# Linformer attention and a squared-ReLU layer: the attention of the next batch in three pieces instead of four, a projection moved up, loads issued earlier

## The chip, the cores and the metric

The kernel runs on one core of a Trainium2 chip. The metric is the device time of one execution in microseconds (us). The kernel before takes 484.29 us, the median of 4 runs (483.24 to 484.89).

## What is computed

Inputs are q, k, v of 8 batches x 8 heads x 1024 rows x 64, two projection matrices E and F (64 x 1024), and the weights of a two-layer network (512 x 2048 and 2048 x 512), all float32.

```python
k_proj = np.einsum('ks,bhsd->bhkd', E, k)
v_proj = np.einsum('ks,bhsd->bhkd', F, v)
scores = scale * np.matmul(q, k_proj.transpose(0, 1, 3, 2))
scores = scores - np.max(scores, axis=-1, keepdims=True)
attn = np.exp(scores)
attn = attn / (np.sum(attn, axis=-1, keepdims=True) + 1e-09)
attn_out = np.matmul(attn, v_proj)
...
x = np.ascontiguousarray(attn_out.transpose(0, 2, 1, 3)).reshape(B * S, H * D)
h = np.maximum(x @ w_in, 0.0)
return (h * h @ w_out).astype(np.float32)
```

Keys and values are projected from 1024 rows to 64, so attention is small: nearly all matmul work is in the two products of the network, over 8192 rows.

## The kernel before

**The network sets the frame.** For each of the 8 batches, `ffn_groups` returns a list of small functions, "groups", which the main loop at the end calls one after the other. A batch's 1024 rows go in two chunks. A chunk's first product (16 groups, line 489) multiplies xT by w_in into PSUM tiles; ScalarE takes the relu (lines 543 and 545), VectorE squares it into `hsq` (line 553). Its second product (line 509) is done with a scheme of seven block products instead of eight: p1 to p7, each 256 columns wide, with combined weights T1 to T4 and combined operands `s` (VectorE, line 503). Products gather in two PSUM accumulators called y and x/z; ScalarE copies partial results out (line 633), VectorE adds them into the output tile `o_sb` (line 639), and SP stores it. In batches 2 to 6, groups 0 to 15 are the first product of chunk 0, 16 to 30 its second product in the order p1a, p2a, p1b, p1c, p2b, p6, p5, p7, p3, p4 (from p6 on, two groups each), 31 to 46 the first product of chunk 1, and 47 to 61 its second. `before` says how many of the eight products of p2 go into p2a, ahead of p1b; the rest are p2b. z takes the bank of x in these batches, and p6 and p7 take that of y.

**Attention rides between the groups.** The attention of batch b+1 is cut into steps, and a table says ahead of which group of batch b each step is issued: BATCH_1 while batch 0 runs, BATCH_2 while batch 1 runs, PIECES after that. Scores (line 234, four matmuls on 64-row tiles that share the array) go to a PSUM tile; ScalarE takes their exponentials (line 241); sums and values (line 249) are matmuls on 64x32 tiles; logs and inverses (lines 261, 264) give 1/sum on ScalarE; normalize (line 274) writes xT on VectorE. The projection of K and V (lines 207 and 208) fills all 128 rows; its result is copied out by `copy_kp` (VectorE, two copies, and a transposing DMA on SP that makes kT), `copy_vp` (ScalarE, two copies) and `copy_v_down` (VectorE). `transpose_q` is a transposing DMA on SP that makes qT. A second set of tables, AHEAD and AHEAD_1, places projection, copies and transpose_q of the batch after the next.

**Order and buffers.** Each engine executes its instructions in the order in which the program issues them, waiting only on data and on buffers. From batch 2 on, PSUM holds three attention tiles of two banks each, which scores, sums, values and every second first-product tile take in turn, and two single banks, which the other first-product tiles and y, x/z take in turn. K_sb, V_sb, Q_sb and qT have one buffer each, the other projection results two, the output tiles two. Loads are issued on GpSimd (line 108) and change the type from float32 to bfloat16 on the way; transposes and stores are issued on SP. Both queues are executed in order. A load waits until the buffer's last reader is done.

**Where loads stand.** The main loop calls `load_batch(b + 2)` ahead of group 35 of batch 0, 14 of batch 1, and 1 of the others; batch 1's loads are at group 31 of batch 0. The order is Q, K, V but for batch 1.

Of the kernel before, what the change touches and what calls it, by code (L numbers as in the profile page):

```python
# [8 lines left out]
P = 128  # L9
F32 = mybir.dt.float32  # L10
BF16 = mybir.dt.bfloat16
# [9 lines left out]
def kernel(  # L21
# [13 lines left out]
    B, H, S, D = q.shape  # L35
    KP = E.shape[0]
    C = H * D
# [5 lines left out]
    NCB = C // P  # L43
    NFB = FF // P
    HFB = NFB // 2
    NT = NI // 2
# [14 lines left out]
    x_pool = ctx.enter_context(tc.tile_pool(name="x", bufs=2))  # L61
# [17 lines left out]
    def regroup_psum():  # L79
        mixed_stack.close()  # L80
        ffn_home.clear()
        for pool in mixed:
            ffn_pools.remove(pool)
        att_pools.append(mixed_stack.enter_context(psum_pool("mps", 1)))

    def att_psum(shape, dtype):
        pool = att_pools.pop(0)
        att_pools.append(pool)
        return pool.tile(shape, dtype, tag="att", name="ps_att")

    def ffn_psum(name, shape=(P, 512), dtype=F32):

        pool = ffn_home[name] = ffn_pools[0]
        used(name)
        return pool.tile(list(shape), dtype, tag="ffn", name=name)

    def used(name):
        pool = ffn_home.get(name)
        if pool:
            ffn_pools.remove(pool)  # L100
            ffn_pools.append(pool)
# [4 lines left out]
    def load(name, src, b):  # L106
        t = qkv_pool.tile([P, H, NI * D], BF16, name=name)
        nc.gpsimd.dma_start(t[:], rows(src, b))  # L108
        return t

    e_f32 = []
    for src in (E, F):
        t = relu_pool.tile([KP, S], F32, tag="h_relu", name="e_f32")
        nc.sync.dma_start(t[:], src[:])
        e_f32.append(t)
    K_first, V_first, Q_first = (
        qkv_pool.tile([P, H, NI * D], BF16, name=n) for n in ("K_sb", "V_sb", "Q_sb"))
# [46 lines left out]
    def E_and_F():  # L164
        for t, src, copy in ((ET, e_f32[0], nc.vector.tensor_copy), (FT, e_f32[1], nc.scalar.copy)):
            e_bf = soft_pool.tile([KP, S], BF16, tag="expT", name="e_bf")
            copy(e_bf[:], src[:])
            ps = ffn_psum("ps_E", (P, NI, KP), BF16)
            view = e_bf[:].rearrange("k (p i) -> k i p", i=NI)
            for i in range(NI):  # L170
                nc.tensor.transpose(ps[:, i, :], view[:, i, :], ident[0:KP, 0:KP])
            copy(t[:], ps[:])
# [7 lines left out]
    def combine_weights(q4, name):  # L180
        js = slice(4 * q4, 4 * q4 + 4)
        o, a, b = {"T1": (T1, W12, W11), "T2": (T2, W22, T1), "T3": (T3, W22, W12), "T4": (T4, W21, T2)}[name]
        nc.vector.tensor_tensor(out=o[:, js], in0=a[:, js], in1=b[:, js], op=ALU.subtract)
# [4 lines left out]
    class Attention:  # L188
# [2 lines left out]

        def __init__(self, b, Q, K, V):
            self.Q, self.K, self.V = Q, K, V
            self.xT = x_pool.tile([P, NCB, 2, NT, P], BF16, name="xT")
            self.exp, self.rs, self.ps = {}, {}, {}
            self.qT = qt_pool.tile([P, H * NT, P], BF16, name="qT")

        def transpose_q(self):
            nc.sync.dma_start_transpose(out=self.qT[:], in_=self.Q[:].rearrange("p h c -> p (h c)"))

        def project(self, early=0):
            ps = self.ps["kv"] = ffn_psum("ps_kv") if early else att_psum([P, C], F32)
            kv = self.K[:].rearrange("p h (i d) -> p h i d", i=NI)
            vv = self.V[:].rearrange("p h (i d) -> p h i d", i=NI)
            for i in range(NI):
                f, l = i == 0, i == NI - 1
                nc.tensor.matmul(ps[0:KP, :], lhsT=ET[:, i, :], rhs=kv[:, :, i, :], start=f, stop=l)  # L207
                nc.tensor.matmul(ps[KP:P, :], lhsT=FT[:, i, :], rhs=vv[:, :, i, :], start=f, stop=l)
# [62 lines left out]
            self.ps["v", g, e] = self.quads(g, lambda o, h: self.vp[o, h, e, :])  # L271

        def normalize(self, g, e):
            nc.vector.tensor_tensor(  # L274
                out=self.xT[:, 2 * g + e].rearrange("p a n t -> p a (n t)"),
                in0=self.ps["v", g, e][:], in1=self.rs[g][:], op=ALU.mult,
            )
# [156 lines left out]

    PIECES = {
        18: "scores 0, scores 1, scores 2", 20: "exponentials 0, exponentials 1", 21: "exponentials 2",
        23: "scores 3, exponentials 3",
        27: "sums 0, sums 1, values 0 0, reciprocals 0", 28: "reciprocals 1", 29: "normalize 0 0",  # L440
        49: "values 0 1, values 1 0, values 1 1", 51: "normalize 0 1", 53: "normalize 1 0",
        55: "normalize 1 1",
    }

    AHEAD = {23: "project", 24: "copy_kp", 25: "copy_vp", 26: "copy_v_down", 33: "transpose_q"}
    AHEAD_1 = {33: "transpose_q", 53: "project 1", 58: "copy_kp", 59: "copy_vp", 61: "copy_v_down"}
    BATCH_1 = {
        33: "project 1", 34: "copy_kp, transpose_q, copy_vp", 37: "copy_v_down",
# [7 lines left out]
    BATCH_2 = {  # L456
        12: "project 1", 13: "copy_kp, transpose_q", 14: "copy_vp", 17: "copy_v_down",
# [5 lines left out]
    }  # L463
    SECOND_HALF = {
# [16 lines left out]
    def calls(table, n):  # L481
        for c in filter(None, table.get(n, "").split(", ")):
            name, *args = c.split()
            yield name, [int(a) for a in args]

    def ffn_groups(b, xT):
# [30 lines left out]
        def chunk(ch):  # L517
# [93 lines left out]
            lo, hi = range(0, 4), range(4, 8)  # L611


            before = lo if b == B - 1 else range(3 if b == 1 else 2)

            ALL = slice(0, 2)

# [96 lines left out]
                    nc.sync.dma_start(out_rows[b, ch, 1, :, tb, 0:MH], st["o1"][:, tb, 0:MH])  # L714

            lohi = lambda p: [lambda: p(lo), lambda: p(hi)]
            if b == B - 1:
                (p5a, p5b), rest = lohi(p5), lohi(p7) + lohi(p3)
                second = [p1a, p2a, p5a, p1b, p1c, p2b] + lohi(p6) + [p5b] + rest
            elif b > 1:  # L720
                second = [p1a, p2a, p1b, p1c, p2b] + lohi(p6) + lohi(p5) + lohi(p7) + lohi(p3)
            else:
                second = [p1a, p2a, p1b, p1c] + lohi(p5) + lohi(p6) + lohi(p3) + lohi(p7) + [p2b]
            second += [p4_last] if last else lohi(p4)
            return steps, second, begin_sums, operands

        (f0, s0, begin0, operands0), (f1, s1, begin1, operands1) = chunk(0), chunk(1)
        if b:
            return f0 + s0 + f1 + s1
# [15 lines left out]


    with tc.manual_schedule(engines=ORDERED):
        def load_batch(b):

            if b < B:  # L750
                order = [("K_sb", k), ("V_sb", v), ("Q_sb", q)] if b == 1 else [("Q_sb", q), ("K_sb", k), ("V_sb", v)]
                t = {n: load(n, src, b) for n, src in order}
                return Attention(b, t["Q_sb"], t["K_sb"], t["V_sb"])

        E_and_F()
        cur = Attention(0, Q_first, K_first, V_first)
        cur.first_stages()
        nxt = ahead = None
        for b in range(B):
            for n, g in enumerate(ffn_groups(b, cur.xT)):  # L760
                if b == 0:
                    for name, args in calls(SECOND_HALF, n):
                        getattr(cur, name)(*args)
                    for name, args in calls(WEIGHTS, n):
                        combine_weights(args[0], name)
                    if n == 31:
                        nxt = load_batch(1)
                if nxt:
                    for name, args in calls((BATCH_1, BATCH_2, PIECES)[min(b, 2)], n):
                        getattr(nxt, name)(*args)  # L770
                    if n == (35, 14, 1)[min(b, 2)]:
                        ahead = load_batch(b + 2)
                if b and ahead:
                    for name, args in calls(AHEAD_1 if b == 1 else AHEAD, n):
                        getattr(ahead, name)(*args)
                g()
            if b == 0:
                nxt.normalize(1, 1)
            if b == 1:
                regroup_psum()  # L780
            cur, nxt, ahead = nxt, ahead, None


# [28 lines left out]
```

The softmax here doesn't subtract the row's maximum and nothing guards it: scores larger than these inputs give would overflow.

## Time and profile before

The profiled execution took 484.71 us; its span, first to last instruction, is 482.9 us, with a granted TensorE clock of 1.000. The table adds rows of the page and of the groups by shape that the prediction does not show. Busy times of different engines overlap; idle is the time that the engine stood still just before these instructions.

| group | count | busy us | mean ns | idle before, us |
|---|---|---|---|---|
| first product, 128x512, both PSUM kinds (L489) | 1024 | 238.5 | 379 | 0.2 |
| scores (L234) | 112 | 9.0 | 389 | 0.1 |
| projection into an attention tile (L207, L208) | 64 | 15.4 | 382 | 0.0 |
| projection into a single bank (L207, L208) | 48 | 11.4 | 382 | 0.0 |
| values (L249, expT, vp) | 224 | 8.9 | 380 | 0.3 |
| squares on VectorE (L553) | 123 | 150.1 | 1223 | 79.8 |
| exponentials, 128x1024 (L241) | 28 | 27.5 | 1043 | 1.8 |
| loads of K, V, Q on GpSimd (L108) | 21 | 18.5 | 880 | mostly Q, 252.8, for the transpose of the Q before |

A matmul's mean is its latency; because matmuls overlap, what one costs in a stream is the distance between starts. In the list of DMAs, K takes a median of 14.8 us from issue to landing, V 21.7, Q 10.2, a store of 512 KB 3.2, a transpose of Q 7.7 and one of K 2.6. Batch 2's first product starts at 143.48 us, that of batch 3 at 200.63 and that of batch 4 at 257.77.

### The profile page before, as it was taken

The numbers are of one execution on the slowest core, as the hardware profiler recorded it, in microseconds if no ns is written. First come the engines' busy times: TensorE is split into PE (matmuls) and PEld (weight loads), VectorE is DVE, ScalarE is ACT, GpSimd is POOL, SyncE is SP. The second block draws the span as 40 slices with busy tenths as digits, with TensorE's granted clock in tenths as the row PEclk, the third lists the DMA queues.
The fourth block names the chain that finished last, engine by engine and source line by source line (L and its number), as shares of the span: only waits on it lengthen the run. The fifth ranks groups of instructions, "written<-read, shape, count | busy, mean of one in ns | idle before, by whom it ended". The sixth has DMA issues, their size and how long they took to land.

```text
span 482.9 us, 8401 instructions
## 1 busy us (share of the span) xinstructions
PE 470.4 (97%) x3630; PEld 294.1 (61%) x3630; DVE 314.6 (65%) x382; ACT 246.9 (51%) x365; POOL 34.9 (7%) x48
## 2 busy tenths in 40 slices
PE   3899999999999999999999999999999999999997
PEld 2544677475574756757476664846658475766656
DVE  1468955563967659584694937858486755949383
ACT  2377635758516574357633566155652666334352
POOL 6440020020020002000110002000000000000000
PEclk9999999999999999999999999999999999999999
DMA  9999989669989268900797027950521002020202
GB/s 153 203 204 207 158 186 194 148 108 212 172 142 239 34 164 133 228 1 12 174 173 178 0 65 132 197 143 1 132 54 65 24 1 88 1 89 0 88 1 87
DMA packets 72789, 55.46 MB, mean 115 GB/s; under 512 B 33968, under 2 KB 64944, under 8 KB 72752
## 3 DMA queue, kind: packets, MB, share of 16 engines
q0 software_dynamic: 30624, 29.36, 38.4%
q1 hardware_dynamic: 42128, 25.56, 20.3%
q8 instruction: 28, 0.46, 0.4%
q14 instruction: 9, 0.07, 0.1%
HBM read 59.24 MB, written 16.78 MB: 157 GB/s over the span
## 4 chain that ended last, share of the span: by engine, by line
PE 92%; DVE 4%; ACT 2%; DMA 2%; issue 0%; ACTq 0%; POOLq 0%
PE ps_h L489 27%; PE ps_y L509 21%; PE ps_att L489 17%; PE ps_z L509 15%; PE ps_att L509 2%; PE ps_att L249 2%; DMA K_sb<-in_k_dram 2%; PE ps_att L234 2%; PE ps_att L207 2%; DVE hsq L553 1%; PE ps_x L509 1%; DVE s L503 1%; PE ps_k L290 1%; PE ps_kv L207 1%; ACT h_relu L543 1%; DVE xT L274 0%
## 5 line engine op out<-in xcount | busy, mean ns | idle before, releaser
L553 DVE TENSOR_TENSOR hsq<-h_relu 128x1024 bf16<-128x1024 f32 x123 | 150.1, 1223 | 79.8 <-ACT h_relu L545 63.2
L489 PEld LDWEIGHTS <-w_in 128*128 128x128 bf16 x1024 | 99.7, 98 | 117.7 <-issue 1.9
L489 PE MATMUL ps_h<-xT,w_in 128*128 128x512 bf16 x640 | 147.8, 379 | 0.2 <-DVE xT L379 0.2
L509 PEld LDWEIGHTS <-s 128*128 128x128 bf16 x1024 | 98.8, 98 | 18.4 <-issue 6.5
L543 ACT ACTIVATE h_relu<-ps_h 128x512 f32<-128x512 f32 x159 | 92.4, 596 | 24.2 <-PE ps_h L489 23.9
L489 PE MATMUL ps_att<-xT,w_in 128*128 128x512 bf16 x384 | 90.7, 379 | 0.0
L509 PEld LDWEIGHTS <-hsq 128*128 128x128 bf16 x768 | 73.8, 98 | 18.1 <-issue 7.5
L545 ACT ACTIVATE h_relu<-ps_att 128x1024 f32<-128x1024 f32 x48 | 49.1, 1023 | 55.2 <-PE ps_att L489 55.2
L509 PE MATMUL ps_y<-T,s 128*128 128x256 bf16 x480 | 57.7, 273 | 0.1
L503 DVE TENSOR_TENSOR s<-hsq 128x1024 bf16<-128x1024 bf16 x64 | 43.6, 685 | 0.0
L274 DVE TENSOR_TENSOR xT<-ps_att,rs 128x1024 bf16<-128x1024 f32 x28 | 33.4, 1218 | 0.7 <-PE ps_att L249 0.7
L639 DVE TENSOR_TENSOR o_sb<-ps_z,p_b 128x512 f32<-128x512 f32 x16 | 11.1, 692 | 32.3 <-PE ps_z L509 27.2
L509 PE MATMUL ps_y<-w_out,hsq 128*128 128x256 bf16 x240 | 31.2, 273 | 0.0
L509 PE MATMUL ps_z<-T,s 128*128 128x256 bf16 x256 | 31.0, 273 | 0.0
L509 PE MATMUL ps_z<-w_out,s 128*128 128x256 bf16 x256 | 30.6, 273 | 0.0
L633 ACT COPY o_sb<-ps_y 128x512 f32<-128x512 f32 x15 | 8.7, 579 | 40.8 <-PE ps_y L509 40.6
L509 PE MATMUL ps_y<-T,hsq 128*128 128x256 bf16 x240 | 29.0, 273 | 0.0
L241 ACT ACTIVATE expT<-ps_att 128x1024 bf16<-128x1024 f32 x28 | 27.5, 1043 | 1.8 <-PE ps_att L234 1.8
L633 ACT COPY p_a<-ps_y 128x512 f32<-128x512 f32 x15 | 8.8, 586 | 32.1 <-PE ps_y L509 32.1
L108 POOL DMA_DIRECT2D Q_sb<-in_q_dram x7 | 6.1, 876 | 252.8 <-DMA qT<-Q_sb 251.6
L503 DVE TENSOR_TENSOR s<-s,hsq 128x1024 bf16<-128x1024 bf16 x32 | 21.9, 688 | 0.5
L503 DVE TENSOR_TENSOR s<-hsq,s 128x1024 bf16<-128x1024 bf16 x32 | 21.9, 686 | 0.0
(90 smaller groups left out, 284.6 us busy)
## 6 DMA issues: line engine op xcount, KB each, us to landing
out_dram<-o_sb SPq DMA_DIRECT2D x30, 512.0 KB, 3.2
K_sb<-in_k_dram POOLq DMA_DIRECT2D x7, 1024.0 KB, 14.8
V_sb<-in_v_dram POOLq DMA_DIRECT2D x7, 1024.0 KB, 21.7
Q_sb<-in_q_dram POOLq DMA_DIRECT2D x7, 1024.0 KB, 10.2
w_out<-in_moe_w_out_dram POOLq DMA_DIRECT2D x4, 512.0 KB, 13.2
w_in<-in_moe_w_in_dram POOLq DMA_DIRECT2D x7, 256.0 KB, 10.1
K_sb<-in_k_dram POOLq DMA_DIRECT2D x2, 512.0 KB, 9.1
out_dram<-o_sb SPq DMA_DIRECT2D x3, 256.0 KB, 2.1
```

Source lines behind the costliest of these rows:

```text
L207: nc.tensor.matmul(ps[0:KP, :], lhsT=ET[:, i, :], rhs=kv[:, :, i, :], start=f, stop=l)
L234: nc.tensor.matmul(ps[o, bank, :], lhsT=self.kT[r, 2 * pr + j, :], start=True, stop=True, rhs=self.qT[r, NT * (2 * pr + j):NT * (2 * pr + ...
L241: nc.scalar.activation(e[:], self.ps["s", pr][:], AF.Exp, scale=SCALE)
L274: nc.vector.tensor_tensor(out=self.xT[:, 2 * g + e].rearrange("p a n t -> p a (n t)"), in0=self.ps["v", g, e][:], in1=self.rs[g][:], op=AL ...
L489: nc.tensor.matmul(ps[:], lhsT=w_in_blk(cb, fb), rhs=xT[:, cb, :, 2 * ch:2 * ch + 2], start=(cb == 0), stop=(cb == NCB - 1),)
L503: nc.vector.tensor_tensor(out=s[o][:, js], in0=x, in1=y, op=op)
L509: nc.tensor.matmul(ps[tb] if len(ps) == 2 else ps[0][:, tb], lhsT=lhs[:, j, tb * P:(tb + 1) * P], rhs=rhs[:, j], start=first and n == 0 an ...
L543: nc.scalar.activation(r[:, n], ps[:], AF.Relu)
L545: nc.scalar.activation(r[:], st["h"][:], AF.Relu)
L553: multiply = lambda: nc.vector.tensor_tensor(out=o, in0=r[:], in1=r[:], op=ALU.mult)
L633: nc.scalar.copy(to[:, t], ps)
L639: nc.vector.tensor_tensor(out=to[:, t], in0=ps, in1=more[:, t], op=ALU.add)
```

## The change

The tables now name steps of two batches: a plain name is a step of batch b+1, a name with "+" one of batch b+2, and they replace AHEAD and AHEAD_1. Batches are kept in a dictionary. In the middle batches (2 to 5, table PIECES) scores 0 to 2, the projection for batch b+2 and scores 3 are all issued ahead of group 16, and the projection goes to a single bank instead of an attention tile; the copies follow there too, and transpose_q moves from group 33 to group 21. Batch 6 has its own table, LAST_PIECES, with the old places. In batches 2 to 5 the second product of chunk 0 starts p1a, p1b, p1c, p2a, p2b instead of p1a, p2a, p1b, p1c, p2b. In batch 1, values 1 and the projection move from group 53 to 55, and normalize 1 0 and 1 1 from 54 and 55 to 56 and 59. `before` is 4 instead of 2 in batch 0's second chunk and 4 instead of 3 in batch 1. Loads of batch 4 move to group 56 of batch 1, and those of b+3 to group 30 of batch b, in the order K, V, Q (Q, K, V for batches 2 and 3). xT and qT are taken from their pools when first written instead of with the load.

```diff
+        def begin_qT(self):
+            self.qT = qt_pool.tile([P, H * NT, P], BF16, name="qT")
+
+        def begin_xT(self):
             self.xT = x_pool.tile([P, NCB, 2, NT, P], BF16, name="xT")
...
         def transpose_q(self):
+            self.begin_qT()
             nc.sync.dma_start_transpose(out=self.qT[:], in_=self.Q[:].rearrange("p h c -> p (h c)"))
 
-        def project(self, early=0):
-            ps = self.ps["kv"] = ffn_psum("ps_kv") if early else att_psum([P, C], F32)
+        def project(self, in_ffn_bank=0):
+            ps = self.ps["kv"] = ffn_psum("ps_kv") if in_ffn_bank else att_psum([P, C], F32)
...
         def normalize(self, g, e):
+            if not self.xT:
+                self.begin_xT()
...
     PIECES = {
+        16: "scores 0, scores 1, scores 2, exponentials 0, +project 1, scores 3, exponentials 1, "
+            "+copy_vp, exponentials 2, +copy_kp",
+        19: "exponentials 3", 20: "+copy_v_down", 21: "+transpose_q",
+        27: "sums 0, sums 1, values 0 0, reciprocals 0", 28: "reciprocals 1", 29: "normalize 0 0",
+        49: "values 0 1, values 1 0, values 1 1", 51: "normalize 0 1", 53: "normalize 1 0",
+        55: "normalize 1 1",
+    }
+    LAST_PIECES = {
         18: "scores 0, scores 1, scores 2", 20: "exponentials 0, exponentials 1", 21: "exponentials 2",
         23: "scores 3, exponentials 3",
...
-    AHEAD = {23: "project", 24: "copy_kp", 25: "copy_vp", 26: "copy_v_down", 33: "transpose_q"}
-    AHEAD_1 = {33: "transpose_q", 53: "project 1", 58: "copy_kp", 59: "copy_vp", 61: "copy_v_down"}
...
-        30: "sums 0, sums 1, logs 0", 31: "logs 1", 33: "inverses 0",
-        36: "inverses 1", 47: "values 0 0, values 0 1", 48: "normalize 0 0, normalize 0 1",
-        53: "values 1 0, values 1 1", 54: "normalize 1 0", 55: "normalize 1 1",
+        30: "sums 0, sums 1, logs 0", 31: "logs 1", 
+        33: "+transpose_q, inverses 0", 36: "inverses 1", 47: "values 0 0, values 0 1", 48: "normalize 0 0, normalize 0 1",
+        55: "values 1 0, values 1 1, +project 1", 56: "normalize 1 0",
+        58: "+copy_kp", 59: "+copy_vp, normalize 1 1", 61: "+copy_v_down",
     }
...
-            before = lo if b == B - 1 else range(3 if b == 1 else 2)
+            before = range(2) if (b, ch) == (0, 0) or 1 < b < B - 1 else lo
...
-            if b == B - 1:
+            if 1 < b < B - 2 and ch == 0:
+                second = [p1a, p1b, p1c, p2a, p2b] + lohi(p6) + lohi(p5) + lohi(p7) + lohi(p3)
+            elif b == B - 1:
...
+                order = [("K_sb", k), ("V_sb", v), ("Q_sb", q)]
+                order = order[2:] + order[:2] if b in (2, 3) else order
                 t = {n: load(n, src, b) for n, src in order}
-                return Attention(b, t["Q_sb"], t["K_sb"], t["V_sb"])
+                batches[b] = Attention(b, t["Q_sb"], t["K_sb"], t["V_sb"])
+
+        LOADS = {0: {31: 1, 35: 2}, 1: {14: 3, 56: 4}}
...
+            tables = {0: BATCH_1, 1: BATCH_2, B - 2: LAST_PIECES, B - 1: {}}
+            for n, g in enumerate(ffn_groups(b, batches[b].xT)):
...
+                for name, args in calls(tables.get(b, PIECES), n):
+                    of = batches.get(b + (2 if name[0] == "+" else 1))
+                    if of:
+                        getattr(of, name.lstrip("+"))(*args)
+                if n in LOADS.get(b, {30: 0}):
+                    load_batch(LOADS.get(b, {30: b + 3})[n])
                 g()
```

More of the change, by code (lines that the diff above doesn't have):

```diff
@@ L193, in __init__ @@
             self.Q, self.K, self.V = Q, K, V
+            self.xT = None
+            self.exp, self.rs, self.ps = {}, {}, {}
+            if b == 0:
+                self.begin_qT()
[3 more added lines that the diff above has]
+        def begin_xT(self):
             self.xT = x_pool.tile([P, NCB, 2, NT, P], BF16, name="xT")
-            self.exp, self.rs, self.ps = {}, {}, {}
-            self.qT = qt_pool.tile([P, H * NT, P], BF16, name="qT")
         def transpose_q(self):
+            self.begin_qT()
             nc.sync.dma_start_transpose(out=self.qT[:], in_=self.Q[:].rearrange("p h c -> p (h c)"))
-        def project(self, early=0):
-            ps = self.ps["kv"] = ffn_psum("ps_kv") if early else att_psum([P, C], F32)
+        def project(self, in_ffn_bank=0):
+            ps = self.ps["kv"] = ffn_psum("ps_kv") if in_ffn_bank else att_psum([P, C], F32)
             kv = self.K[:].rearrange("p h (i d) -> p h i d", i=NI)
@@ L273, in normalize @@
         def normalize(self, g, e):
+            if not self.xT:
+                self.begin_xT()
             nc.vector.tensor_tensor(
@@ L747 @@
     with tc.manual_schedule(engines=ORDERED):
+        batches = {0: Attention(0, Q_first, K_first, V_first)}
         def load_batch(b):
             if b < B:
-                order = [("K_sb", k), ("V_sb", v), ("Q_sb", q)] if b == 1 else [("Q_sb", q), ("K_sb", k), ("V_sb", v)]
+                order = [("K_sb", k), ("V_sb", v), ("Q_sb", q)]
+                order = order[2:] + order[:2] if b in (2, 3) else order
                 t = {n: load(n, src, b) for n, src in order}
-                return Attention(b, t["Q_sb"], t["K_sb"], t["V_sb"])
+                batches[b] = Attention(b, t["Q_sb"], t["K_sb"], t["V_sb"])
@@ L755 @@
+        LOADS = {0: {31: 1, 35: 2}, 1: {14: 3, 56: 4}}
         E_and_F()
-        cur = Attention(0, Q_first, K_first, V_first)
-        cur.first_stages()
-        nxt = ahead = None
+        batches[0].first_stages()
         for b in range(B):
-            for n, g in enumerate(ffn_groups(b, cur.xT)):
+            tables = {0: BATCH_1, 1: BATCH_2, B - 2: LAST_PIECES, B - 1: {}}
+            for n, g in enumerate(ffn_groups(b, batches[b].xT)):
                 if b == 0:
                     for name, args in calls(SECOND_HALF, n):
-                        getattr(cur, name)(*args)
+                        getattr(batches[0], name)(*args)
@@ L764 @@
                     for name, args in calls(WEIGHTS, n):
                         combine_weights(args[0], name)
[L766 to L775, printed above, removed]
+                for name, args in calls(tables.get(b, PIECES), n):
+                    of = batches.get(b + (2 if name[0] == "+" else 1))
+                    if of:
+                        getattr(of, name.lstrip("+"))(*args)
@@ L776 @@
+                if n in LOADS.get(b, {30: 0}):
+                    load_batch(LOADS.get(b, {30: b + 3})[n])
                 g()
             if b == 0:
-                nxt.normalize(1, 1)
+                batches[1].normalize(1, 1)
             if b == 1:
                 regroup_psum()
-            cur, nxt, ahead = nxt, ahead, None
 _INS = ['q', 'k', 'v', 'E', 'F', 'moe_w_in', 'moe_w_out']
```

## The prediction

> **What bounds the kernel.** I read the page's busy rows first, then the chain of waits, then the chain in order of time over one middle batch.
>
> ```profile
> PE 470.4 (97%) x3630; PEld 294.1 (61%) x3630; DVE 314.6 (65%) x382; ACT 246.9 (51%) x365; POOL 34.9 (7%) x48
> ...
> PE 92%; DVE 4%; ACT 2%; DMA 2%; issue 0%; ACTq 0%; POOLq 0%
> ```
>
> TensorE is busy 97% of the span, sets 92% of the end, and its granted clock is 1.000. In the steady batches (2 to 6) it never waits for data, so time can come only from two places: what TensorE itself loses between matmuls, and the few stalls in batches 0 and 1. The work in matmuls is the same before and after. Here is the chain in batch 3, from the end of its first product (start, us, what):
>
> ```profile
> 214.44 0.91 PE ps_y L509 x8
> 215.35 0.44 PE ps_z L509 x4
> 215.78 0.77 PE ps_att L234 x12
> 216.56 0.98 PE ps_y L509 x8
> ...
> 220.59 0.34 PE ps_att L234 x4
> 220.93 0.33 PE ps_att L207
> ...
> 222.78 1.85 PE ps_z L509 x16
> ```
>
> Undisturbed, 16 matmuls of 256 columns take 1.75 us in this chain (0.109 each), and four score matmuls, which share the array, 0.21. So twelve scores should take 0.64 and take 0.77; the eight ps_y behind them should take 0.87 and take 0.98; four scores alone take 0.34 for 0.21; the first projection matmul 0.33 for 0.21; the 16 ps_z behind the projection 1.85 for 1.75. **Each change of shape on the array costs about 0.12 us.** The first ps_y after the first product also loses 0.04 (0.91 for 0.87).
>
> **Middle batches (2 to 5, new table PIECES).** Before, scores 0 to 2 are a piece of their own (in and out: two changes), and scores 3 with the projection another (in, from one to the other, out: three). After, group 16 issues scores 0, 1, 2, the projection for two batches on, and scores 3 in a row, ahead of p1a. That is in, scores to projection, projection to scores, out: four. One change less is 0.12, and the 0.04 goes because scores, not ps_y, now follow the first product: 0.16 a batch, **0.64 us over four batches**. The change from projection to scores isn't in the trace. It costs between 0 and twice the known one, 0.24; I take 0.12, the row of the opposite direction, and keep 0.04 to 0.28 a batch, 0.16 to 1.1 in all. The Trainium skill (TensorEngine Tiling (Array Packing), Key Properties) says that changing the tiling mode drains TensorE, and its page TensorE: Matmul & The Clock Gate (Single matmul latency) gives some 166 ns as the constant that an isolated matmul pays at full clock. By that rule the sum would be 4 x (0.166 + 0.04) = 0.82; the row says 0.64, and the row decides.
>
> What might wait there instead? ScalarE and VectorE in the same batch:
>
> ```profile
> 214.48 0.60 ACT L543 ACTIVATE h_relu<-ps_h 128x512 f32<-128x512 f32 x1 [0.21 <-PE ps_h L489]
> ...
> 218.05 2.86 ACT L241 ACTIVATE expT<-ps_att 128x1024 bf16<-128x1024 f32 x3
> ```
>
> ```profile
> 217.30 0.69 DVE L503 TENSOR_TENSOR s<-hsq 128x1024 bf16<-128x1024 bf16 x1
> ```
>
> With the same first product, the last relu ends at 215.08. TensorE then does scores 0 to 2 (to 215.21), the projection (to 217.06) and scores 3, which needs exponentials 0 done: 215.08 + 1.0 = 216.1, so 0.95 us early. The projection now takes one of the two small banks; its relu ended at 214.26. p1a to p1c (16 matmuls and the change out, 1.86) run from 217.4 to 219.2. p2a, moved behind p1c, writes the bank that the projection leaves, so it waits for both its copies. ScalarE: exponentials 0 and 1 to 217.0, copy_vp (0.64 for two) after the projection's end, to 217.75. VectorE is busy to 218.0 (the last row above); then the copy of kp, 0.68, to 218.7. That is **0.5 us before p2a wants the bank**: the tightest new wait. Behind the kp copy VectorE holds its short copy (0.28) and the operand of p6's second half, ready at 219.7 and wanted at 221.8. Exponentials 2, and 3 behind p_a's copy, end at 221.0, six us before sums. The twelve scores find their buffers: the third takes that of the last 128x1024 relu, done at 213.77. p5's wait for the o_sb add keeps a margin of 1 us. Everything is covered here.
>
> **Loads half a batch sooner.** K and V of b+3 now follow the projection at once (GpSimd waits for nothing else), Q follows transpose_q, itself moved from group 33 to 21, ahead of both stores on SP. The loads end long before their use in the next batch's group 16, but they fall onto the transposes. SP shows both cases, a transpose under loads and one in quiet:
>
> ```profile
> 115.80 17.51 SPq L199 DMA_TRANSPOSE qT<-Q_sb  x1
> ...
> 231.94 5.76 SPq L199 DMA_TRANSPOSE qT<-Q_sb  x1
> ```
>
> The Trainium skill (DMA: Bandwidth & Descriptors, Issuing engines are not separate DMA queues) has all issuers share the same 16 engines and interleave; that speaks against this edit, and the first row agrees. By the quiet row transpose_q, issued at about 220.3, leaves SP at 226; by the loaded row at 238, and the store that is ready at 229.8 waits 8 us behind it, landing (3.2 us median, 8.5 between batches 1 and 2) by 247 at the latest. Its tile is next written by the add that ran at 249.9. Margin 3 us, so no cost either way; were the transpose 10 us longer, four batches would each lose 7. The transposed Q is wanted a batch later. In batch 2, K and V of batch 4 are wanted at about 158. Their loads start when batch 3's projection ends, near 136.9. By the median landings (Q first 9.3, K 14.4, V 18.7, issued 0.9 apart) the three loads are in 9, 15 and 20 us after the first is issued; K and V go first, so V lands by 154 even with 2 us lost to stores. With Q first, as before, it would have been late. LAST_PIECES and batch 7 are as they were: nothing.
>
> **Batches 0 and 1.** p2a's share of products grows (before = lo): in batch 0's second chunk from 4 to 8 matmuls, in batch 1 from 6 to 8, p2b shrinking as much. In batch 0, scores 2 and 3 stall on exponentials:
>
> ```profile
> 70.67 0.89 PE L234 MATMUL ps_att<-qT,kT 64*64 64x512 bf16 x8
> ```
>
> ```profile
> 69.16 1.94 ACT L241 ACTIVATE expT<-ps_att 128x1024 bf16<-128x1024 f32 x2 [0.64 <-PE ps_att L234]
> ```
>
> From this start to the next product (71.49) are 0.82 us; the same eight scores took 0.56 at 68.70. The stall of 0.26 ends with exponentials 1 at 71.1; four more matmuls ahead are 0.44: gone. p4 behind the shortened p2b then waits for an add that ends near 80.8, wanted at 81.0: still covered. In batch 1's first chunk p5 loses 0.09 (1.84 for 1.75) to its second-half operand; 0.22 more ahead removes it. In its second chunk:
>
> ```profile
> 133.04 0.41 PE L249 MATMUL ps_att<-expT,vp 64*32 64x512 bf16 x8 [0.30 <-DVE xT L274]
> ```
>
> ```profile
> 130.63 2.35 DVE L274 TENSOR_TENSOR xT<-ps_att,rs 128x1024 bf16<-128x1024 f32 x2
> 132.90 0.69 DVE L503 TENSOR_TENSOR s<-s,hsq 128x1024 bf16<-128x1024 bf16 x1
> ```
>
> The eight before start at 132.33, so these are 0.50 late. Moving values 1 and the projection from group 53 to 55 puts p6 there, whose second half needs the operand that VectorE ends at 133.59. TensorE arrives at 133.33: a new stall of 0.3 for one of 0.5. Gain 0.2, between 0 and 0.5. The last normalize, now at group 59, ends about 1 us before batch 2 reads it; its cover gone, each us late would cost one.
>
> **Sum.** 0.64 + 0.26 + 0.09 + 0.20 = 1.19 us. The profiled execution took 484.71 (span 482.9 and 1.8 around it), so it would take 483.5; the median of the runs is 0.42 lower, 484.29, and goes to **483.1**, 0.25% less. What a measurement here can tell from no change is 0.3%, 1.45 us.
>
> **Rivals.**
> - *More goes than the count says* (0.20): the change from projection to scores is nearly free and batch 1 stalls no more: 4 x 0.28 + 0.26 + 0.09 + 0.5 = 2.0, to 482.3. For it: adjacent pieces with 64-row tiles; against: every change in the chain costs the same 0.12.
> - *Pieces don't pay* (0.15): the new order loses its 0.16 to short waits at p2a, as p5 in the second chunk loses 0.07 to the add today. Only batches 0 and 1 gain: 483.7. This is also the case that the change does not do what it says.
> - *p2a's gate decides* (0.10): the chain relu, exponentials 0 and 1, copy_vp, copy of kp is longer than worked out, and TensorE stands at p2a in four batches. It costs from 0.5 us of delay on; at 1.3 us late it is 0.8 a batch, 3.2 in all, minus 1.2: +2.0, 486.3. For it: five steps on two engines in order. Against: every duration has a row.
>
> **How the numbers follow.** The forecast has 0.55 (482.6 to 483.6). The range takes in the first two rivals and the spread of the runs (0.8 each way), and stops short of the third: 482.0 to 484.7. Faster by over 0.3% means below 482.84: most of the first rival and a third of the forecast, 0.37. Slower means above 485.74: the third, 0.09. The rest is 0.54.
>
> **What would show it.** In the new profile: chain rows at group 16 with 12 scores, projection and four scores in a row, the first ps_z of p2a without delay, batch to batch 56.98 instead of 57.14; transposes of 15 us or more on SP in batches 2 to 5, harmless; scores of batch 0 back to 0.56. Wrong would be any wait of TensorE for VectorE at p2a, for K or V in batch 2, or a VectorE add waiting for a store.

## The result and the profile after

The changed kernel takes 483.15 us, the median of 43 runs (481.90 to 484.67); the kernel before, measured again beside it, takes 483.74 (64 runs, 482.73 to 485.65; the first four had a median of 484.29). The ratio is 0.9987, 95% interval 0.9980 to 0.9993: a gain of 0.3 to 1.0 us, under the 0.3% that the prediction set as its bound for a visible change. The profiled execution took 483.05 us, its span 481.3.

```profile
PE 469.9 (98%) x3630; PEld 294.4 (61%) x3630; DVE 314.6 (65%) x382; ACT 247.7 (51%) x365; POOL 34.4 (7%) x48
...
PE 92%; DVE 4%; ACT 2%; DMA 1%; issue 0%; SPq 0%
```

The picture of the page is the same: the same matmuls, TensorE on 92% of the chain. The spans differ by 1.6 us, but half of that isn't the change. The first product starts at 22.32 us before and at 21.51 after, behind input loads that no edit touches; in the twelve profiles of this study it starts anywhere from 20.64 to 22.42. So I count from that first matmul to the end of the span. From there on the middle batches repeat to 0.02 us, and a difference of 0.1 us can be read from one profile, while single runs spread over 3 us.

| part (us) | before | after | middle only | longer p2b | operand first | normalize later |
|---|---|---|---|---|---|---|
| batch 0 | 61.22 | 61.06 | 61.22 | 61.01 | 61.00 | 61.01 |
| batch 1, chunk 0 | 30.08 | 30.05 | 30.08 | 30.08 | 30.08 | 30.08 |
| batch 1, chunk 1 | 29.70 | 29.60 | 29.70 | 29.75 | 29.21 | 29.21 |
| batches 2 to 5, each | 57.15 | 57.01 | 57.01 | 57.01 | 57.01 | 56.93 |
| from the first product to the end | 460.60 | 459.77 | 460.06 | 459.88 | 459.37 | 458.99 |

The parts are counted by starts of matmuls; the columns "middle only" to "normalize later" are kernels of the experiments below. Of the 0.83 us between before and after, 4 x 0.14 = 0.56 are the middle batches and 0.29 batches 0 and 1; the last two batches agree within 0.02.

**Middle batches.** The chain of the changed kernel in batch 3 from the end of the first product, to be laid beside the rows of the prediction (start, us, what):

```profile
213.21 0.77 PE ps_att L243 x12
213.98 0.33 PE ps_kv L216
...
215.83 0.34 PE ps_att L243 x4
216.17 1.85 PE ps_y L527 x16
218.02 1.75 PE ps_z L527 x16
```

Twelve scores, the projection and four scores stand in a row. Scores 3 behind the projection cost 0.34 as they did behind ps_y: the change from projection to scores, which no row of before showed, has the common price of some 0.12. The 16 ps_y pay for the way out (1.85), and the ps_z of p2a follow undelayed (1.75). The two copies that p2a waits for, ScalarE's and VectorE's:

```profile
215.90 0.64 ACT L234 CAST vp<-ps_kv 64x256 bf16<-64x256 f32 x2 [0.22 <-PE ps_kv L217]
```

```profile
216.68 0.68 DVE L223 CAST kp<-ps_kv 64x512 bf16<-64x512 f32 x1
```

In the chain a piece begins where the one before it ends; the start of the instruction itself lies up to 0.17 us earlier. A margin has to be taken on one of these two clocks. By starts, p2a begins here:

```profile
217.86 1.91 PE L527 MATMUL ps_z<-w_out,hsq 128*128 128x256 bf16 x16
```

The copy of kp ends at 217.36, so the margin is 0.5. The prediction had 0.5 as well, but set a time of the chain (219.2) against one from a row of starts (218.7).

**SP and the loads.** SP's queue in batch 3:

```profile
219.51 15.18 SPq L208 DMA_TRANSPOSE qT<-Q_sb  x1
234.78 0.53 SPq L704 DMA_DIRECT2D out_dram<-o_sb  x1
```

The transpose runs under the loads of K and V and holds SP for 15 us instead of 5.8; the store leaves behind it, 6 us after its data was ready. Nobody on VectorE waits for a store. It is late and costs nothing.

**Batches 0 and 1.** In these two batches p2b stands last but one, between p7 and p4. TensorE and VectorE where batch 0's second chunk comes to p4, by start of the instructions, first of the kernel before:

```profile
79.81 1.47 PE L509 MATMUL ps_x<-w_out,hsq 128*128 128x256 bf16 x12
```

```profile
80.06 0.68 DVE L639 TENSOR_TENSOR o_sb<-ps_y,p_d 128x512 f32<-128x512 f32 x1
```

Then of the changed kernel:

```profile
79.19 1.04 PE L527 MATMUL ps_x<-w_out,hsq 128*128 128x256 bf16 x8
80.17 1.03 PE L527 MATMUL ps_y<-T,hsq 128*128 128x256 bf16 x8
```

```profile
79.44 0.68 DVE L657 TENSOR_TENSOR o_sb<-ps_y,p_d 128x512 f32<-128x512 f32 x1
```

Eight matmuls of p2b take 0.87, so p4 could start at 80.06. It writes the bank that this add reads, and the add ends at 80.12; p4 starts 0.05 later, **0.11 late**. From the start of p2b to the end of the add pass 0.93 us in both kernels (79.81 to 80.74, 79.19 to 80.12): twelve matmuls of p2b cover that, eight do not. Batch 1's second chunk has the same picture, and a wait at p6:

```profile
131.47 2.23 PE L527 MATMUL ps_y<-T,s 128*128 128x256 bf16 x16
...
139.53 1.04 PE L527 MATMUL ps_x<-w_out,hsq 128*128 128x256 bf16 x8
140.48 1.91 PE L527 MATMUL ps_y<-T,hsq 128*128 128x256 bf16 x16
```

p6 spans 2.23 instead of 1.91: 0.3 of waiting for the operand of its second half, as forecast. p4 comes 0.95 after the start of p2b instead of 0.87, which is 0.08 late; in the chain p4 has 1.81 instead of 1.75, and in the first chunk 0.94 instead of 0.87.

### The profile page after: what moved, and what is told of

The parts are those of the page before. It is cut to its first block, busy times and chain, and to the rows that moved or that the text cites. A ratio compares the mean times of both kernels' runs of the same rounds, so it can differ in the third digit from the quotient of the medians.

```text
span 481.3 us, 8400 instructions
## 1 busy us (share of the span) xinstructions
PE 469.9 (98%) x3630; PEld 294.4 (61%) x3630; DVE 314.6 (65%) x382; ACT 247.7 (51%) x365; POOL 34.4 (7%) x48
## 4 chain that ended last, share of the span: by engine, by line
PE 92%; DVE 4%; ACT 2%; DMA 1%; issue 0%; SPq 0%
PE ps_h L507 27%; PE ps_y L527 21%; PE ps_att L507 17%; PE ps_z L527 15%; PE ps_kv L216 2%; PE ps_att L527 2%; PE ps_att L258 2%; PE ps_att L243 2%; DVE hsq L571 1%; PE ps_x L527 1%; DVE s L521 1%; DMA e_f<-in_F_dram 1%; PE ps_k L301 1%; ACT h_relu L561 1%; PE ps_fill L400 1%; DVE xT L285 0%
## 5 line engine op out<-in xcount | busy, mean ns | idle before, releaser
L657 DVE TENSOR_TENSOR o_sb<-ps_y,p_d 128x512 f32<-128x512 f32 x15 | 10.4, 691 | 23.1 <-issue 21.3
L651 ACT COPY p_b<-ps_y 128x512 f32<-128x512 f32 x15 | 8.8, 588 | 27.5 <-PE ps_y L527 27.5
## 6 DMA issues: line engine op xcount, KB each, us to landing
V_sb<-in_v_dram POOLq DMA_DIRECT2D x7, 1024.0 KB, 17.5
```

The lines of the kernel that those rows point to most:

```text
L651: nc.scalar.copy(to[:, t], ps)
L657: nc.vector.tensor_tensor(out=to[:, t], in0=ps, in1=more[:, t], op=ALU.add)
```

## The experiments

**Which part gives what.** One kernel has only the edits of the middle batches and the loads, one only those of batches 0 and 1. The first, as edits of the changed kernel:

```diff
-            before = range(2) if (b, ch) == (0, 0) or 1 < b < B - 1 else lo
+            before = lo if b == B - 1 else range(3 if b == 1 else 2)
...
-        55: "values 1 0, values 1 1, +project 1", 56: "normalize 1 0",
-        58: "+copy_kp", 59: "+copy_vp, normalize 1 1", 61: "+copy_v_down",
+        53: "values 1 0, values 1 1, +project 1", 54: "normalize 1 0", 55: "normalize 1 1",
+        58: "+copy_kp", 59: "+copy_vp", 61: "+copy_v_down",
```

> Batches 0 and 1 as in the kernel before, middle batches and loads as changed. Counted from the first matmul of the first product to the end of the span (before 460.6 us, after 459.8), so that the input loads at the start, which differ from run to run, stay out. Theory (pieces pay one change of shape per batch): four batches of 57.0 instead of 57.15, so about 460.0 and a gain of 0.55 on the kernel before. Rival (the pieces gain nothing and batches 0 and 1 made the difference): 460.6.

Measured: batches of 57.01, batches 0 and 1 as before to 0.01, 460.06 from the first product on; 483.42 against 483.89 for the kernel before, ratio 0.9990 (0.9980 to 1.0001). The theory holds: the pieces give their 0.14 a batch alone.

In the other kernel, from the kernel before:

```diff
-            before = lo if b == B - 1 else range(3 if b == 1 else 2)
+            before = range(2) if (b, ch) == (0, 0) or 1 < b < B - 1 else lo
...
-        53: "values 1 0, values 1 1", 54: "normalize 1 0", 55: "normalize 1 1",
+        55: "values 1 0, values 1 1", 56: "normalize 1 0", 59: "normalize 1 1",
...
-    AHEAD_1 = {33: "transpose_q", 53: "project 1", 58: "copy_kp", 59: "copy_vp", 61: "copy_v_down"}
+    AHEAD_1 = {33: "transpose_q", 55: "project 1", 58: "copy_kp", 59: "copy_vp", 61: "copy_v_down"}
```

> The kernel before with only the edits of batches 0 and 1 (p2a of four column blocks, values 1 and projection two groups later). Theory from the two traces: stalls of 0.26, 0.09 and about 0.1 go, and waits of 0.11, 0.07 and 0.06 of p4 for an add come in, because p2b in front of it is shorter; net gain 0.25 to 0.3: 460.3 from the first product on, and middle batches of 57.15. Rival (the prediction's sum, no new wait): gain 0.55, 460.05.

Measured: batch 1 as in the changed kernel (30.05 and 29.60), middle batches 57.15, the ps_x and ps_y rows ahead of batch 1 0.87 and 0.98 as there. But batch 0 took 61.58, and the sum is 460.85: in this execution the first product started earliest of all, at 20.64, and the projection of batch 1, some 33 us later, waited for V and lost 0.5. So the sum as it stands decides nothing; without these 0.5 it is the 460.3 of the theory, and the rows speak for it too. Ratio 0.9993 (0.9985 to 1.0002).

**Is it p2b's length that makes p4 wait?**

```diff
-            before = range(2) if (b, ch) == (0, 0) or 1 < b < B - 1 else lo
+            before = range(2) if (b, ch) == (0, 0) or 1 < b < B - 1 else range(3) if b < 2 else lo
```

> The changed kernel with 3 instead of 4 of the eight products of p2 in p2a of batch 0's second chunk and of batch 1, so that p2b ahead of p4 has 10 matmuls (1.09 us) instead of 8 (0.87). Theory (p4 waits for the add that frees its bank): the waits of 0.11, 0.07 and 0.06 go, while p5 in batch 1 loses up to 0.09 again and the scores of batch 0 up to 0.04: from the first product on 459.65 instead of 459.8. Rival (these rows are not a wait but how p4 is): no change of the ps_y rows, 459.8 to 459.9.

The chain of this kernel in batch 0's second chunk, and its TensorE in batch 1's:

```profile
79.03 1.09 PE ps_x L527 x10
80.12 0.87 PE ps_y L527 x8
```

```profile
132.47 1.05 PE L527 MATMUL ps_y<-T,s 128*128 128x256 bf16 x8 [0.37 <-DVE s L521]
```

p4's wait is gone wherever p2b has ten matmuls (0.87, and 1.75 in batch 1's second chunk). The total did not follow: 459.88 for the expected 459.65, which is where the rival had it. With two matmuls less ahead of it, TensorE comes 0.22 sooner to p6's second half, whose operand VectorE delivers when it delivers it, and p6 waits 0.54 in all instead of 0.31 (from its first matmul to the first of values 1 pass 2.38 and 2.15 us; without a wait, in the next kernel, 1.84). The mechanism was right and the expected total wrong: what is saved ahead of a wait is paid at the wait. Ratio 0.9989 (0.9979 to 1.0000).

**Is it VectorE's order that makes p6 wait?** From the last kernel:

```diff
-        33: "+transpose_q, inverses 0", 36: "inverses 1", 47: "values 0 0, values 0 1", 48: "normalize 0 0, normalize 0 1",
+        33: "+transpose_q, inverses 0", 36: "inverses 1", 47: "values 0 0, values 0 1", 49: "normalize 0 0, normalize 0 1",
...
-                    operands(1, (1,) if b > 1 else (1, 3, 2))
+                    operands(1, (1,) if b > 1 or ch else (1, 3, 2))
...
             def p1b():
+                if b == 1 and ch:
+                    operands(1, (3, 2))
```

> As the kernel with the longer p2b, and in batch 1's second chunk VectorE computes the operand of p6's second half ahead of normalize 0 0 and 0 1 instead of behind them. Theory (p6 waits 0.3 to 0.4 us for this operand): the wait goes and no other comes, 459.3 from the first product on. Rival (values 1, which need the buffers that the two normalizes free, then wait instead): values 1 late by 0.3 or more, 459.6.

VectorE in batch 1's second chunk, first of the changed kernel, then of this one; the operand is `s<-s,hsq`, the two normalizes are `xT`:

```profile
129.64 2.35 DVE L285 TENSOR_TENSOR xT<-ps_att,rs 128x1024 bf16<-128x1024 f32 x2
131.91 0.68 DVE L521 TENSOR_TENSOR s<-s,hsq 128x1024 bf16<-128x1024 bf16 x1
```

```profile
129.22 0.69 DVE L521 TENSOR_TENSOR s<-s,hsq 128x1024 bf16<-128x1024 bf16 x1
129.83 2.35 DVE L285 TENSOR_TENSOR xT<-ps_att,rs 128x1024 bf16<-128x1024 f32 x2
```

TensorE in the same chunk of this kernel:

```profile
130.70 1.91 PE L527 MATMUL ps_y<-T,s 128*128 128x256 bf16 x16
132.54 0.63 PE L258 MATMUL ps_att<-expT,vp 64*32 64x512 bf16 x16
```

p6 runs in one go (1.91), and values 1 follow without a wait. The chunk takes 29.21 instead of 29.75, the total is 459.37, and the time 482.23 against 483.89: ratio 0.9970 (0.9959 to 0.9980). One of this chunk's two normalizes is 1.2 us on VectorE, the operand 0.7; the operand was wanted first.

The operand's edit without the longer p2b:

> The changed kernel with only the operand of p6's second half ahead of the two normalizes in batch 1's second chunk; p2b as short as in the changed kernel. Theory: p6's wait of 0.3 to 0.4 goes, p4's short waits of 0.11, 0.07 and 0.06 stay: 459.4 from the first product on, batch 1's second chunk 29.2. Rival (the longer p2b is needed for the gain): 459.6 or more.

Measured: batch 1's second chunk 29.28, of which p4's 0.06 are most of the rest to 29.21; p4's rows 0.98, 0.94 and 1.81 as in the changed kernel. Batch 0 took 61.36 in this execution, 0.30 more than in the changed kernel although nothing in it differs. These 0.30 were lost ahead of its projection: 0.24 of them in the first 4.3 us of the first product, where two matmuls wait for w_in (a part of it landed at 25.66 us instead of 25.02). The total is 459.75, and 459.45 without the 0.30, for 459.4 in the theory. Ratio 0.9976 (0.9963 to 0.9989).

**Was p2a's move needed?**

```diff
-                second = [p1a, p1b, p1c, p2a, p2b] + lohi(p6) + lohi(p5) + lohi(p7) + lohi(p3)
+                second = [p1a, p2a, p1b, p1c, p2b] + lohi(p6) + lohi(p5) + lohi(p7) + lohi(p3)
```

> The changed kernel with the old order p1a, p2a, p1b, p1c, p2b in the middle batches. Theory (p2a needs the bank that the projection leaves, free when the copy of kp ends, at 217.3 us in batch 3 by the changed kernel's trace; p2a would be ready at 217.15): a wait of 0.1 to 0.3 us in each of four batches, batches of 57.1 to 57.3, so the gain of the pieces is gone or turned round. Rival (the gate has room, the reordering was not needed): batches of 57.0.

In batch 3 of this kernel (which starts 1.2 us later than that of the changed kernel: 0.8 from the beginning and 0.4 from the wait in batch 2), TensorE and VectorE:

```profile
218.64 0.60 PE L527 MATMUL ps_z<-w_out,hsq 128*128 128x256 bf16 x4 [0.26 <-DVE kp L223]
```

```profile
217.91 0.68 DVE L223 CAST kp<-ps_kv 64x512 bf16<-64x512 f32 x1
```

The wait for the copy of kp is there, in all four batches, which take 57.43: 0.42 longer than in the changed kernel and 0.28 longer than before. That is more than the expected 0.1 to 0.3, because the expectation mixed clocks as well: 217.15 is a time of the chain, some 0.16 behind the start, and the copy's end (217.36) and 0.05 for the handover give 0.42. (The 0.26 in the row counts from the modelled end of the matmul before.) In all 461.46 from the first product on, 0.9 more than before; ratio 1.0008 (0.9992 to 1.0023). The place is that of the prediction's third rival, and the new order of the second product is what keeps the wait out. Its chain of five steps over ScalarE is not what sets it: the copy follows VectorE's own queue (squares and operands until 217.9).

**What do the loads matter?** First the order Q, K, V in all batches from 2 on:

```diff
-                order = order[2:] + order[:2] if b in (2, 3) else order
+                order = order[2:] + order[:2] if b > 1 else order
```

> The changed kernel with the loads of every batch from 2 on in the order Q, K, V. Theory: in batch 2 V of batch 4 lands about 159.5 us instead of 154.5, and the projection, which reached the array at 156.9, waits 2.5 to 3 us once; in batches 3 to 5 K and V start only after the transpose of Q, which then runs in quiet (5 to 6 us on SP instead of 15), and nothing of that shows in the time: batches of 57.0. In all about 2.7 slower than the changed kernel. Rival (loads have room in any order): no difference.

TensorE in batch 2 and SP in that batch:

```profile
159.49 0.38 PE L217 MATMUL ps_kv<-V_sb,FT 128*64 128x512 bf16 x1 [1.41 <-DMA V_sb<-in_v_dram]
```

```profile
164.41 4.76 SPq L208 DMA_TRANSPOSE qT<-Q_sb  x1
```

The projection waits for V once, and the stretch from the middle of batch 1 to the middle of batch 2 takes 61.37 instead of 59.58: 1.8 us, where I had expected 2.5 to 3. V landed at 159.44 as expected, but in this execution the projection came to the array 0.8 us later (157.67 for 156.9). Transposes run in quiet (4.7 to 5.2 us on SP), and the batches keep their 57.01. So the loads under which SP's transposes triple cost nothing, and the only thing in the order is batch 2. Ratio 1.0006 (0.9990 to 1.0022).

Then the old place of the calls, with the new order:

```diff
-        LOADS = {0: {31: 1, 35: 2}, 1: {14: 3, 56: 4}}
+        LOADS = {0: {31: 1, 35: 2}, 1: {14: 3}}
...
-                if n in LOADS.get(b, {30: 0}):
-                    load_batch(LOADS.get(b, {30: b + 3})[n])
+                if n in LOADS.get(b, {1: 0}):
+                    load_batch(LOADS.get(b, {1: b + 2})[n])
```

> The changed kernel with the loads placed in the program as before (group 1 of the batch that projects them), in the new order K, V, Q. Theory: GpSimd issues only loads here, and each starts when its buffer is free, wherever the program names it; issue times within 0.5 us of the changed kernel's and the same time, 459.8 from the first product on. Rival (half a batch sooner matters): K and V of batch 5 issued some 30 us later than 159.1, the projection of a middle batch waiting for them.

GpSimd's loads of batch 5, first in the changed kernel, then in this one (whose first product started 0.9 us later):

```profile
159.11 0.88 POOL L108 DMA_DIRECT2D K_sb<-in_k_dram  x1 [20.10 <-PE ps_kv L217]
```

```profile
160.02 0.88 POOL L108 DMA_DIRECT2D K_sb<-in_k_dram  x1 [20.10 <-PE ps_kv L217]
```

Each starts when the projection has read the buffer, wherever the program names it. The total is 459.73, ratio 0.9985 (0.9970 to 0.9999): the new place of the calls is worth nothing. In the kernel before, K of batch 5 was issued at 183.85, behind Q, which waits for its transpose; in the changed kernel with Q first at 172.52. What brings it to 159.11 is the earlier projection and K ahead of Q.

**What does one change of shape cost?** Scores 3 one group later:

```diff
-        16: "scores 0, scores 1, scores 2, exponentials 0, +project 1, scores 3, exponentials 1, "
+        16: "scores 0, scores 1, scores 2, exponentials 0, +project 1, exponentials 1, "
             "+copy_vp, exponentials 2, +copy_kp",
+        17: "scores 3",
```

> The changed kernel with scores 3 one group later, behind p1a, so that they are a piece of their own again (one change of shape more per batch: out of the projection, into and out of scores 3, instead of projection to scores and out). Theory (0.12 us per change): batches of 57.12 to 57.15, 0.5 in all. Rival (what pays is not the number of changes but that the pieces come ahead of the second product): batches of 57.0.

Its chain in batch 3:

```profile
216.34 0.98 PE ps_y L528 x8
217.32 0.34 PE ps_att L243 x4
217.66 0.98 PE ps_y L528 x8
```

The eight ps_y now pay twice (0.98 for 0.87). Batches take 57.11 to 57.12: 0.10 for one change more, a little under the expected. The kernel before has as many changes of shape and takes 57.15; the 0.04 between the two is the prediction's small term, that scores and not ps_y follow the first product. The sum, 460.69, holds another 0.5 in batch 0, where the projection waited for V in this execution:

```profile
54.16 0.38 PE L217 MATMUL ps_kv<-V_sb,FT 128*64 128x512 bf16 x1 [0.35 <-DMA V_sb<-in_v_dram]
```

Ratio 0.9988 (0.9974 to 1.0001).

**A better version.** In every second chunk of the middle batches p5 has 1.82 instead of 1.75 in the chain, before and after. It writes the bank that the add of x reads. From the kernel with the operand first, in PIECES and LAST_PIECES:

```diff
-        49: "values 0 1, values 1 0, values 1 1", 51: "normalize 0 1", 53: "normalize 1 0",
+        49: "values 0 1, values 1 0, values 1 1", 52: "normalize 0 1", 53: "normalize 1 0",
```

> As the kernel with the longer p2b and the operand first, and in the second chunk of batches 2 to 6 normalize 0 1 one group later, behind the add of x. Theory (the 1.82 instead of 1.75 us of p5 in each second chunk is a wait for that add, which stands behind normalize 0 1 on VectorE): 0.07 in each of five batches, second chunks of 26.96 instead of 27.03, 459.05 from the first product on; 0.3 to 0.4% faster than the kernel before. Rival (the 0.07 is in how p5 starts): chunks of 27.03, 459.4.

The chain and VectorE in batch 3, first of the changed kernel, then of this one:

```profile
249.34 1.82 PE ps_z L527 x16
```

```profile
248.52 0.68 DVE L657 TENSOR_TENSOR o_sb<-ps_z,p_a 128x512 f32<-128x512 f32 x1
```

```profile
248.63 1.75 PE ps_z L527 x16
```

```profile
246.97 0.69 DVE L657 TENSOR_TENSOR o_sb<-ps_z,p_a 128x512 f32<-128x512 f32 x1 [0.21 <-PE ps_z L527]
```

By starts, p5 begins at 248.46, 0.8 us after the end of the add; in the changed kernel it begins at 249.26, 0.06 after that end. p5 loses nothing now. Second chunks take 26.95, the total is 458.99, as the theory had it. The time is 482.31 against 483.49 for the kernel before, ratio 0.9970 (0.9954 to 0.9985). By the profile it beats the kernel before by 1.61 us and the changed kernel by 0.78. The 0.38 that this last step adds to the kernel with the operand first is read from the profiles alone: the ratios of the two are the same.

## Why the prediction came out as it did

The forecast of 483.1 us met the measured 483.15 by luck: the kernel before measured 483.74 in more runs, 0.55 under the median from which the forecast was counted. The change itself was forecast at 1.19 us and gave 0.6 by the medians (0.3 to 1.0) and 0.83 by the profiles.

- *What bounds the kernel*: right. No engine but TensorE comes into the chain of a middle batch, before or after.
- *One change of shape less*: right in kind, a little too large: 0.14 a batch for 0.16, 0.56 for 0.64. By the run with scores 3 apart, 0.10 of the 0.14 is the change of shape (0.12 in the forecast) and 0.04 the small term, as forecast. The unknown price of projection to scores was taken from the opposite direction, and that is what it costs (0.34 for 0.21). The 0.10 is near the row's 0.12 and well below the 166 ns that the Trainium skill gives as the constant of an isolated matmul (TensorE: Matmul & The Clock Gate, Single matmul latency) and that the prediction tried as the price of a change: the row was the better guide.
- *p2a's gate*: covered, with 0.5 of margin on one clock. The forecast's 0.5 mixed two, so its size is luck. Without p2a's move the gate decides, at 0.42 a batch.
- *Loads under transposes*: right. SP held for 15 us (17.5 taken), the store late, landing at 238.0 (247 at the latest in the forecast), nobody waiting. V of batch 4 in time with K and V first, and late with Q first, by 1.8 us.
- *Batches 0 and 1*: here the sum was wrong, 0.29 for 0.55. The stalls removed were sized rightly: scores 2 and 3 of batch 0 are back at 0.56, p5 of batch 1 at 1.75, p6's new wait is 0.3. What failed is the step "p4 behind the shortened p2b then waits for an add that ends near 80.8, wanted at 81.0: still covered". It was not covered, and batch 1's two chunks, where p2b is shortened as well, were not looked at for it at all: 0.11 + 0.07 + 0.06 = 0.24 us. The 81.0 is a time of the chain, which here stands 0.17 behind the start of the instruction (p2b 79.98 and 79.81 before), and the 80.8 fits a row of starts (the add ends at 80.74 before). A margin of 0.2 from two clocks was none. On one clock the rows of before give the wait itself: the add ends 0.93 after the start of p2b, the handover to the matmul takes 0.05, and eight matmuls cover 0.87 of that, which leaves the 0.11 that was measured. The run with the longer p2b shows the cause (the waits go), and with the operand first and the longer p2b together these batches give 0.22 + 0.49 = 0.71 instead of 0.29.

## What to carry to other kernels

When one engine is busy throughout, count its changes of shape and the short waits of its instructions on buffers; here 0.1 us each, times batches, was all that was left, and one profile showed it where dozens of runs hardly did. A product that is shortened to give cover in one place loses it in another: look up who comes behind it and for which reader of its bank it waits, and compare both on the same clock, since the chain's times and the starts differ. And a time saved ahead of a wait is only moved to that wait: take away the wait (here by the order of VectorE's queue) first.

## What the runs showed of the hardware

The start of the first product varied by 1.8 us over twelve profiles of kernels with the same beginning. In two of them V of batch 1, loaded behind the weights, landed at 53.35 and 54.12 us, 0.7 after TensorE had begun with K, which made batch 0 0.5 us longer; in a third the weights w_in were late, which cost 0.24. A transpose of 1 MB held SP for 4.7 to 5.9 us in quiet and 13.9 to 18.0 us beside loads. From the end of an add on VectorE to the start of the matmul that waited for it 0.05 to 0.06 us passed. What makes the start vary was not tried and stays open.
